# A retention kernel with two mixtures of experts: raw weights of expert 0 loaded one at a time and split row by row, mixed x kept one step later

## Chip, cores and metric

The kernel runs on one core of a Trainium2 chip. The metric is the time of one execution on the device in microseconds (us); lower is better. The engines are TensorE (PE, with its weight loads as PEld), VectorE (DVE), ScalarE (ACT), GpSimd (POOL) and SyncE (SP, which here only starts transfers).

## What is computed

Three stages on 2304 tokens of width 512: a retention layer (attention with a decay per head, without softmax), a dense mixture of 4 experts, and a mixture of 8 experts of which each token takes one.

```python
scores = scale * np.matmul(q, k.transpose(0, 1, 3, 2))
Dmat = np.where(rel >= 0, gamma[:, None, None] ** rel[None, :, :], 0.0)
x = np.matmul(scores * Dmat, v)                 # 4 x 8 heads x 576 x 64, then 2304 x 512
for e in range(4):                              # first mixture, dense
    out += p[:, e:e + 1] * (np.maximum(x @ w1[e], 0.0) @ w2[e])
for e in range(8):                              # second mixture, one expert a token
    out[mask] = gate_w[mask, None] * eom[mask, e, None] * (np.maximum(x[mask] @ w1[e], 0.0) @ w2[e])
```

All inputs and outputs are float32; the large matmuls run as sums of float16 products, each operand split into a high and a low part.

## The kernel before

**Retention.** 4 sequences of 9 chunks of 64 tokens make 36 steps s. A step (`at_step`, L394) has four groups of small matmuls on PE: the product with the state (L300), the scores of the next step (L277), the scores times v (L309) and what the next state gains (L324). DVE makes from them the masked scores `pf` (L282), the new state `sn` (four rows, L341, or one copy, L336) and x, as `xf` (L358). There is one PSUM buffer for scores (`sc`) and one for products (`uo`), so PE's next L277 waits for `pf`, and its next L300 for `xf`. `at_parts` splits `xf` into a high (ACT, L365) and a low part (POOL, L366) in `xo`. POOL also makes `ks`, the scaled keys (L256).

**Token blocks.** Four steps fill a block b of 256 tokens, of which there are 9. `x_mix` (L373, POOL, two calls of two rows) forms differences of x in place; `x_keep` splits them into `xm` (ACT L384, POOL L385; one buffer for each half, or straight into `xc` for blocks 0 and 1), and `x_store` writes parts to DRAM from POOL (L390, L392). `ago(s, b)` counts the steps since block b was filled; mixing falls on 1 and 2, keeping on 3 and 4, each with its store.

**Expert 0 in blocks 0 to 4.** A block has four units of the first layer (`l1_first`, L559, 24 matmuls into `ph`, then `ht` on ACT L545 and DVE L546) and four of the second (`l2`, L711, 12 matmuls into `po`). In blocks 1 to 3 the list has 8 units u = 0 to 7, l1 first; block 0 has only its four l2 units (its l1 is in the opening), block 4 only its four l1 units (its l2 goes with block 5). Behind each unit stands a call of `at_hook` (one retention step; in block 0 two behind every second unit), then `w_plan`. From block 5 on, and for experts 1 to 3, a scheme with 7 products of half size is used (`l1_mixed`, `l2_mixed`), for which the weights are mixed too.

**The weights.** Raw weights of an expert are eight loads of 128 x 1024 float32 (0.5 MB each, `w_load`, on SP) into four buffers `wr`: 0 to 3 of w1, 4 to 7 of w2. For the early blocks they are loaded and split once at the start (`w_split`; the form `split` uses ACT and DVE, `split_p` ACT, ACT and POOL). For the scheme of block 5 they are loaded again and go through a list of steps, `w_todo`, one taken by `w_do` behind each unit: `mix` writes a difference or sum back to `wr` (ACT L487 to a PSUM tile `pz`, DVE L488), `put` splits a quarter (ACT L219 to `pz`, ACT L220, DVE L221). The two k in the lists are two rows of blocks of a weight: k = 0 of w1 needs loads 0 and 2, k = 1 loads 1 and 3; of w2 4 and 6, then 5 and 7. Before, the list starts behind (0, 2) with the loads of w1 as two steps, 12 steps of w1 with k alternating, an empty step, two steps of loads of w2 and 10 steps of w2.

**What sets the order.** Up to L1208 the program's order holds on each engine. From L1209 on a scheduler orders each engine's instructions by what they depend on; `tc.issue_after` holds an instruction behind a named one of its engine. Each engine runs its own list in order and waits where an operand isn't there.

## Time and profile before

| | before |
|---|---|
| median of 3 runs | 1001.67 us (999.87 to 1007.35) |
| the profiled execution | 1003.75 us, of which 1001.9 are the span from first to last instruction |
| PE busy | 963.7 us (96%) |
| DVE, ACT, POOL busy | 574.1, 535.7, 421.2 us |
| mean granted TensorE clock | 0.992 |
| DMA | 209.49 MB, 209 GB/s in the mean |

The page cuts the span into 40 slices and gives each engine's busy share in tenths:

```profile
PE   6988999999999999999999999999999999999994
PEld 5565667899999999999999999999987677777773
DVE  5664572466667777766777675888888111211210
ACT  3354463667758777766777686676642122221211
POOL 4677674555556234455342454342322221112111
PEclk9999999999999999999999999999999999999997
DMA  9687884336556777457668726888834616654690
```

A slice is 25 us. A 9 is 90% or more. In the first six slices all engines and the DMA engines are in use; later PE alone is full. A wait is shown in brackets behind an instruction, with what released it; "issue" means that nothing in the profile accounts for it.

### The profile page before, as it was taken

To read this page: it belongs to the slowest core of one execution; us is meant where nothing else is said; L and a number is where in the kernel's file an instruction comes from. 1 tells how busy PE (TensorE), PEld (TensorE's weight loads), DVE (VectorE), ACT (ScalarE), POOL (GpSimd) and SP (SyncE) were. 2 spreads that over 40 slices of the span, in tenths; PEclk is the share of its full clock that TensorE was granted. 3 is DMA by queue.
4 is the path that set the end of the run, shared out by engine and by line. 5 is a ranking of instruction groups with operands and counts; after the bars stand their busy time and mean duration, and the time that the engine had idled before them with its cause. 6 is when DMAs were issued, how large, how long until landed. Compare 5 with 4: busy or idle time off the path is not lost. (4 is left out here: it accounts for less than half of the span.)

```text
span 1001.9 us, 31931 instructions
## 1 busy us (share of the span) xinstructions
PE 963.7 (96%) x13507; PEld 827.1 (83%) x13507; DVE 574.1 (57%) x1290; ACT 535.7 (53%) x1019; POOL 421.2 (42%) x446
## 2 busy tenths in 40 slices
PE   6988999999999999999999999999999999999994
PEld 5565667899999999999999999999987677777773
DVE  5664572466667777766777675888888111211210
ACT  3354463667758777766777686676642122221211
POOL 4677674555556234455342454342322221112111
PEclk9999999999999999999999999999999999999997
DMA  9687884336556777457668726888834616654690
GB/s 353 232 307 248 280 283 170 112 103 199 165 185 193 246 258 252 155 191 215 205 198 306 258 77 169 255 211 235 228 122 189 232 43 229 216 206 162 256 387 34
DMA packets 96052, 209.49 MB, mean 209 GB/s; under 512 B 21598, under 2 KB 42334, under 8 KB 93600
## 3 DMA queue, kind: packets, MB, share of 16 engines
q1 hardware_dynamic: 82784, 159.20, 47.7%
q0 software_dynamic: 13120, 48.20, 15.1%
q8 instruction: 108, 1.77, 0.7%
q14 instruction: 40, 0.33, 0.1%
HBM read 197.88 MB, written 52.99 MB: 250 GB/s over the span
## 5 line engine op out<-in xcount | busy, mean ns | idle before, releaser
L672 PEld LDWEIGHTS <-op 128*128 128x128 f16 x2604 | 245.7, 98 | 26.0 <-POOL s L211 0.7
L606 POOL TENSOR_TENSOR op<-sm,op 128x512 f16<-128x512 f32 x124 | 142.3, 1159 | 225.8 <-ACT op L605 225.7
L587 PEld LDWEIGHTS <-wm_a 128*128 128x128 f16 x3264 | 192.8, 98 | 3.9
L587 PE MATMUL ph<-xc,wm_a 128*128 128x128 f16 x2112 | 132.2, 219 | 0.0
L605 ACT ACTIVATE op<-sm 128x512 f16<-128x512 f32 x124 | 77.5, 634 | 86.6 <-DVE sm L610 85.1
L1094 DVE SCALAR_TENSOR_TENSOR h_s<-p_h,h_s 128x512 f16<-128x512 f32 x40 | 27.7, 691 | 159.5 <-ACT h_s L1093 159.5
L1101 PE MATMUL p_y<-wm_a,h_s 128*128 128x512 f16 x480 | 107.2, 379 | 0.5 <-DVE h_s L1094 0.5
L672 PE MATMUL pv<-wm_a,op 128*128 128x256 f16 x792 | 97.4, 273 | 0.0
L672 PE MATMUL px<-wm_a,op 128*128 128x256 f16 x744 | 91.3, 272 | 0.7 <-DVE acc L680 0.7
L1101 PEld LDWEIGHTS <-h_s 128*128 128x128 f16 x480 | 46.7, 98 | 52.3 <-DVE h_s L1094 0.7
L221 DVE TENSOR_TENSOR s<-pz,s 128x512 f16<-128x512 f32 x111 | 73.9, 682 | 15.6 <-ACT s L220 15.6
L1104 POOL DMA_INDIRECT out_dram<-y_s,sidxm x17 | 17.3, 1019 | 146.3 <-ACT y_s L1103 129.2
L587 PEld LDWEIGHTS <-wm_b 128*128 128x128 f16 x1296 | 76.9, 98 | 1.4
L219 ACT ACTIVATE pz<-sr 128x512 f32<-128x512 f32 x111 | 65.6, 605 | 15.0 <-DVE rk L830 7.9
L490 POOL TENSOR_TENSOR wr<-wr 128x512 f32<-128x512 f32 x48 | 60.5, 1271 | 29.8 <-ACT pz L219 29.1
L1093 ACT ACTIVATE h_s<-p_h 128x512 f16<-128x512 f32 x40 | 23.9, 597 | 79.6 <-PE p_h L1084 75.4
L220 ACT ACTIVATE s<-pz 128x512 f16<-128x512 f32 x111 | 64.0, 599 | 0.6
L1103 ACT ACTIVATE y_s<-p_y,x_g 128x512 f32<-128x512 f32 x20 | 13.7, 687 | 92.5 <-PE p_y L1101 78.9
L680 DVE SCALAR_TENSOR_TENSOR acc<-px,p_sb,acc 128x256 f32<-128x256 f32 x124 | 59.1, 476 | 6.8 <-PE px L672 6.5
L1084 PEld LDWEIGHTS <-wm_b 128*128 128x128 f16 x1056 | 59.9, 98 | 3.3 <-issue 1.1
L1084 PE MATMUL p_h<-x_s,wm_b 128*128 128x128 f16 x1056 | 61.6, 219 | 0.7 <-issue 0.7
L221 DVE TENSOR_TENSOR wm_a<-pz,wm_a 128x512 f16<-128x512 f32 x62 | 42.0, 688 | 34.7 <-ACT wm_a L220 34.3
(231 smaller groups left out, 1814.7 us busy)
## 6 DMA issues: line engine op xcount, KB each, us to landing
wm_a<-w2d SPq DMA_DIRECT2D x20, 2048.0 KB
wr<-in_w_dram SPq DMA_DIRECT2D x40, 512.0 KB
wm_b<-w1d SPq DMA_DIRECT2D x10, 2048.0 KB
wm_a<-w1d SPq DMA_DIRECT2D x10, 2048.0 KB
sr<-in_w1s_dram SPq DMA_DIRECT2D x64, 256.0 KB
w1d<-s SPq DMA_DIRECT2D x64, 256.0 KB
sr<-in_w2s_dram SPq DMA_DIRECT2D x64, 256.0 KB
w2d<-s SPq DMA_DIRECT2D x64, 256.0 KB
```

The source lines that it names most:

```text
L219: act.activation(out=z, in_=raw, func=ACTF.Copy, scale=scale)
L220: act.activation(out=hi, in_=z, func=ACTF.Copy)
L221: dve.tensor_tensor(out=lo, in0=z, in1=hi, op=ALU.subtract)
L490: pace["pool"] = pool.tensor_tensor(out=quarter(e, n, k, to), in0=quarter(e, n, k, x), in1=quarter(e, n, k, y), op=op)
L587: pe.matmul(bank[:, i], lhsT=w[:, k, u, 128 * i:128 * i + 128], rhs=x[:, v, d, k], start=(first and i == 0 and n == 0), stop=(n == 5), ski ...
L605: act.activation(out=hi, in_=s, func=ACTF.Copy)
L606: pool.tensor_tensor(out=lo, in0=s, in1=hi, op=ALU.subtract)
L672: pe.matmul(out, lhsT=o[a][:, v, k], rhs=w[c][:, k, u], start=(first and n == 0), stop=(n == 11), skip_group_check=True,)
L680: step = dve.scalar_tensor_tensor(out=a, in0=src, scalar=p_sb[:, b * TB + i, e:e + 1], in1=a, op0=ALU.mult, op1=ALU.add)
L1084: pe.matmul(ph[:, j], lhsT=w[k][:, x, f * 128:(f + 1) * 128], rhs=xs[:, y, k], start=(n == 0), stop=(n == 3 * KD - 1),)
L1094: dve.scalar_tensor_tensor(out=lo, in0=ph, scalar=0.0, in1=hi, op0=ALU.max, op1=ALU.subtract)
L1101: pe.matmul(po, lhsT=h[:, a, k], rhs=w[k][:, b], start=(n == 0), stop=(n == 3 * KF - 1))
```

## The change

Four things are changed. Expert 0's steps of w1 and w2 run all of k = 0 and then all of k = 1. Its eight raw loads are no longer steps of the list: `RAW_AT` names for each the unit behind which it is asked for, and the list of 22 steps starts behind (1, 4). `x_keep` and the stores behind it move from 3 and 4 steps after a block's last to 4 and 5 (the hook runs to one step more, with two calls behind (4, 3)). And in the opening, the split of the second row of w2 moves ahead of two retention steps.

```diff
--- before.py
+++ after.py
@@ -511,14 +511,16 @@
                 lambda q=q: q(0, 4),
                 lambda q=q: q(2, 6),
             ]
-        return [f for pair in zip(*rows) for f in pair]
+        return rows[0] + rows[1] if e == 0 else [f for pair in zip(*rows) for f in pair]
 
     def w2_steps(e):
         steps = []
 
+        late = []
+
         def both(*what):
             for k in range(2):
-                steps.append(lambda k=k: [w(k) for w in what])
+                (late if k and e == 0 else steps).append(lambda k=k: [w(k) for w in what])
 
         q = lambda i, c: lambda k: put(e, 1, k, i, c)
         m = lambda to, x, y: lambda k: mix(e, 1, k, to, x, y, ALU.subtract)
@@ -533,7 +535,7 @@
         both(q(3, 2), m(2, 2, 3))
         both(q(1, 4))
         both(q(2, 6))
-        return steps
+        return steps + late
 
 
     hts = {}
@@ -1195,11 +1197,11 @@
     w_split(0, KD)
     at_split(NS + 1)
     l1_first(0, 1, 1, 2)
+    w_split(0, KD + 1, split_p)
     later_step(NS)
     at_scores(NS + 1)
     l1_first(0, 2, 1, 2)
     later_step(NS + 1)
-    w_split(0, KD + 1, split_p)
     at_split(NS + 2)
     l1_first(0, 3, 1, 2)
     w_split(0, KD + 2)
@@ -1232,7 +1234,7 @@
 
     def at_hook():
         s = nxt[0]
-        if s >= NSTEP + 4:
+        if s >= NSTEP + 5:
             return
         nxt[0] += 1
         if s + 4 < NSTEP:
@@ -1265,13 +1267,13 @@
             if n == 2:
                 x_store(b, 0)
                 x_mix(b, 1)
-            if 2 < n < 5:
-                x_keep(b, n - 3)
+            if 3 < n < 6:
+                x_keep(b, n - 4)
                 if b > 1:
-                    x_store(b, n - 1)
-            if b < 2 and n == 5:
+                    x_store(b, n - 2)
+            if b < 2 and n == 6:
                 x_store(b, 1)
-        if s == NSTEP + 3:
+        if s == NSTEP + 4:
             at_ctx.close()
             wm["b"] = ctx.enter_context(tc.tile_pool(name="w_b", bufs=1)).tile([128, 6, 2048], F16, name="wm_b")
             later["raw"] = ctx.enter_context(tc.tile_pool(name="raw_s", bufs=3))
@@ -1308,13 +1310,19 @@
                 pend_store.append(s_split(i - 2, f))
         s_at[0] = i + 1
 
+    RAW_AT = {(0, 3): 0, (1, 1): 2, (1, 3): 1, (1, 5): 3, (2, 3): 4, (2, 5): 6, (3, 0): 5, (3, 2): 7}
+
     def w_plan(e, b, u):
 
         if e == 0 and b < BM:
-            if (b, u) == (0, 2):
-                w_todo.extend([w_loads(0, 0, 2), w_loads(0, 1, 3)] + w1_steps(0) + [lambda: None])
-                w_todo.extend([w_loads(0, 4, 6), w_loads(0, 5, 7)] + w2_steps(0))
-            w_do()
+            if (b, u) == (0, 3):
+                w_todo.extend(w1_steps(0) + w2_steps(0))
+            i = RAW_AT.get((b, u))
+            if i is not None:
+                with tc.issue_after(pace["sp"].ins):
+                    w_load(0, i)
+            if (b, u) >= (1, 4):
+                w_do()
         elif e < 3 and b >= (2 if e else BM):
             if (b, u) == (2 if e else BM, 0):
                 w_tiles(e + 1)
@@ -1417,7 +1425,7 @@
                     with tc.issue_after(pace["pool"].ins):
                         x_load((b + 1) % NB, pool)
                 if e == 0:
-                    for _ in range(1 + (b == 0 and u % 2)):
+                    for _ in range(1 + (b == 0 and u % 2 or (b, u) == (BM - 1, 3))):
                         at_hook()
                 if not last:
                     w_plan(e, b, u)
```

In SP's list, the start of the second raw loading (`wr<-in_w_dram`; `qkr` and `vkr` are the inputs of a retention step) before:

```order
L450 DMA wr<-in_w_dram 128x1024 x2
L248 DMA vkr<-in_vk_dram 128x640
L242 DMA qkr<-in_qk_dram 128x640 x2
L450 DMA wr<-in_w_dram 128x1024
L248 DMA vkr<-in_vk_dram 128x640
L450 DMA wr<-in_w_dram 128x1024
L248 DMA vkr<-in_vk_dram 128x640
L242 DMA qkr<-in_qk_dram 128x640 x2
L248 DMA vkr<-in_vk_dram 128x256
```

and after:

```order
L450 DMA wr<-in_w_dram 128x1024
L248 DMA vkr<-in_vk_dram 128x640
L242 DMA qkr<-in_qk_dram 128x640
L248 DMA vkr<-in_vk_dram 128x640
L242 DMA qkr<-in_qk_dram 128x640
L450 DMA wr<-in_w_dram 128x1024
L248 DMA vkr<-in_vk_dram 128x256
L242 DMA qkr<-in_qk_dram 128x640
L248 DMA vkr<-in_vk_dram 128x640
L242 DMA qkr<-in_qk_dram 128x512
L450 DMA wr<-in_w_dram 128x1024
```

The four loads that stood among two steps' inputs now stand one by one among the inputs of several; the first of them is where the third was.

In ACT's list, around the end of block 1's units (`xm_` with a number is one half of one block's mixed x: 1617 and 1616 are block 3's before, 1663 the first half of block 3 after), before:

```order
L219 ACTIVATE pz<-wr 128x512
L384 ACTIVATE xm_1617<-xf 128x512
L365 ACTIVATE xo<-xf 128x4x64
L384 ACTIVATE xm_1616<-xf 128x512
L220 ACTIVATE wm_a<-pz 128x512
L219 ACTIVATE pz<-wr 128x512
L220 ACTIVATE wm_a<-pz 128x512
```

and after:

```order
L384 ACTIVATE xm_1396<-xf 128x512
L487 ACTIVATE pz<-wr 128x512 x3
L365 ACTIVATE xo<-xf 128x4x64
L219 ACTIVATE pz<-wr 128x512
L220 ACTIVATE wm_a<-pz 128x512
L487 ACTIVATE pz<-wr 128x512
L219 ACTIVATE pz<-wr 128x512
L365 ACTIVATE xo<-xf 128x4x64
L384 ACTIVATE xm_1663<-xf 128x512
L220 ACTIVATE wm_a<-pz 128x512
```

The first half of block 3 stands one retention step later, behind an `xo` and with one L220 behind it instead of four rows of x and weights; block 2's second half (1396) and the first steps of the weight list have come into the rows ahead of it.

In DVE's list, from the unit (2, 3) on (the `ht` row is its first), before:

```order
L546 SCALAR_TENSOR_TENSOR ht<-ph,ht 128x512
L282 TENSOR_TENSOR pf<-sc,ka 128x256
L206 SCALAR_TENSOR_TENSOR wg_sb<-wgr,wg_sb 128x64
L341 SCALAR_TENSOR_TENSOR sn<-sn,ka,uo 128x64 x4
L358 TENSOR_TENSOR xf<-uo,ka 128x4x64
L221 TENSOR_TENSOR wm_a<-pz,wm_a 128x512
L282 TENSOR_TENSOR pf<-sc,ka 128x256
L341 SCALAR_TENSOR_TENSOR sn<-sn,ka,uo 128x64 x4
L358 TENSOR_TENSOR xf<-uo,ka 128x4x64
```

and after, from the second row behind that unit's `xf`:

```order
L221 TENSOR_TENSOR wm_a<-pz,wm_a 128x512
L488 TENSOR_TENSOR wr<-pz,wr 128x512
L221 TENSOR_TENSOR wm_a<-pz,wm_a 128x512
L282 TENSOR_TENSOR pf<-sc,ka 128x256
L221 TENSOR_TENSOR wm_a<-pz,wm_a 128x512
L341 SCALAR_TENSOR_TENSOR sn<-sn,ka,uo 128x64 x4
L358 TENSOR_TENSOR xf<-uo,ka 128x4x64
L221 TENSOR_TENSOR wm_a<-pz,wm_a 128x512
```

Between the `xf` of one step and that of the next stood one L221; now four rows of the weight steps stand there (and the gate weights' L206 ahead of them), and one more behind.

## Rows read from the trace of the kernel before

**Rows 1.** Stretches: busy us of each engine, granted clock, DMA share, GB/s.

```profile
50.00:75.00 25.00, 21.63 (x467) 16.77 (x458) 15.19 (x46) 12.91 (x26) 19.08 (x28) 0.93 0.86 307
...
400.00:450.00 50.00, 50.00 (x683) 47.46 (x682) 35.35 (x60) 35.36 (x68) 26.23 (x25) 1.00 0.53 176
```

**Rows 2.** PE's timeline, 30 to 68 us: start, us, operation, [wait <-releaser].

```profile
34.69 0.59 PE L711 MATMUL po<-wm_c,ht 128*128 128x512 f16 x2 [0.83 <-POOL wm_c L139]
...
37.19 0.46 PE L277 MATMUL sc<-qkr 64*64 64x64 f32 x16 [0.48 <-DVE pf L282]
...
54.14 0.33 PE L309 MATMUL uo<-pf,vkr 64*64 64x64 f32 x5 [1.35 <-issue]
...
62.48 0.40 PE L300 MATMUL uo<-qkr,sn 64*64 64x64 f32 x11 [1.94 <-issue]
...
63.69 1.46 PE L559 MATMUL ph<-xc,wm_c 128*128 128x256 f16 x6
...
67.16 0.82 PE L559 MATMUL ph<-xc,wm_a 128*128 128x256 f16 x6
```

**Rows 3.** Instruction queue's packets in 51.75:52, 60:60.25, 63.5:63.75: count, MB, share.

```profile
q8 instruction: 1, 0.02, 24.2%
...
q8 instruction: 1, 0.02, 25.1%
...
q8 instruction: 1, 0.02, 38.5%
```

**Rows 4.** A stretch behind the second "issue" wait, columns as rows 1.

```profile
64.00:66.00 2.00, 2.00 (x11) 1.35 (x10) 1.96 (x7) 0.42 (x1) 1.66 (x4) 0.50 0.96 257
```

**Rows 5.** PE's timeline, 85 to 154 us.

```profile
85.60 0.46 PE L277 MATMUL sc<-qkr 64*64 64x64 f32 x16 [2.67 <-DVE pf L282]
...
86.35 0.46 PE L309 MATMUL uo<-pf,vkr 64*64 64x64 f32 x16 [0.29 <-DVE xf L358]
...
86.98 4.45 PE L711 MATMUL po<-wm_a,ht 128*128 128x512 f16 x12
...
119.80 0.46 PE L300 MATMUL uo<-qkr,sn 64*64 64x64 f32 x16 [1.08 <-DVE xf L358]
...
139.26 0.46 PE L300 MATMUL uo<-qkr,sn 64*64 64x64 f32 x16 [0.57 <-DVE xf L358]
...
141.16 0.46 PE L277 MATMUL sc<-qkr 64*64 64x64 f32 x16 [0.74 <-DVE pf L282]
142.36 2.75 PE L711 MATMUL po<-wm_c,ht 128*128 128x512 f16 x12 [0.73 <-DVE wr L488]
...
153.16 0.46 PE L300 MATMUL uo<-qkr,sn 64*64 64x64 f32 x16 [0.71 <-DVE xf L358]
```

**Rows 6.** Timelines of ACT (two rows), POOL and SP (two rows).

```profile
28.80 0.42 ACT L139 ACTIVATE xc<-xf 128x256 f16<-128x256 f32 x1 [2.53 <-DVE xf L139]
...
81.43 0.63 ACT L384 ACTIVATE xm<-xf 128x512 f16<-128x512 f32 x1 [2.94 <-DMA xcd<-xm]
...
74.97 0.68 POOL L392 DMA_DIRECT2D xcd<-xm  x1 [0.30 <-POOL xm L385]
...
43.81 1.64 SPq L450 DMA_DIRECT2D wr<-in_w_dram  x2
...
51.44 0.45 SPq L450 DMA_DIRECT2D wr<-in_w_dram  x1
```

**Rows 7.** Groups by line, 40 to 168 us: count, busy us, mean ns, idle before.

```profile
L373 POOL TENSOR_TENSOR xf<-xf 128x256 f32<-128x256 f32 x35 | 26.6, 760 | 4.2 <-DVE xf L358 3.1
...
L341 DVE SCALAR_TENSOR_TENSOR sn<-sn,ka,uo 128x64 f32<-128x64 f32 x84 | 17.8, 273 | 3.4 <-PE uo L324 3.2
...
L385 POOL TENSOR_TENSOR xm<-xf,xm 128x512 f16<-128x512 f32 x13 | 15.2, 1177 | 6.7 <-ACT xm L384 6.6
...
L221 DVE TENSOR_TENSOR wm_a<-pz,wm_a 128x512 f16<-128x512 f32 x14 | 9.6, 686 | 8.0 <-ACT wm_a L220 7.8
```

**Rows 8.** Transfers that write or read x's parts in DRAM, 40 to 170 us.

```profile
DMA to landing us min/median/max: 2.5/5.3/8.6
```

## Prediction

> **What bounds the kernel now.** I read the stretches first. From 200 us on TensorE (PE) is busy without a gap (400 to 450: 50.00 of 50); only the opening and the first five token blocks leave it idle, 3.4 us in 50 to 75 [rows 1]. The change moves work in those blocks alone, so its gain is at most the idle time there. The program's order on PE differs in three places by one group of rows; what changes is when the others serve it. I then listed, in PE's timeline, every wait between 30 and 157 us with its releaser [rows 2, 5], and asked of each whether the change moves what it waits for. A unit is one step of block b's l1 or l2 list, written (b, u), followed by one retention step; a pair takes about 3.85 us.
>
> The waits: 0.83 and 0.48 at 34 to 37 us; 1.35 and 1.94 "issue" at 54 and 62; 2.67 and 0.29 at 85.6; 1.08 at 119.8; 0.57, 0.74, 0.73 and 0.71 at 139 to 153 [rows 2, 5]. Two of them cost more: behind the 1.94 the granted clock is 0.50 (1.2 of 2.4 GHz) [rows 4], and behind the 2.67 the matmuls are as slow. Four groups of six lasted from 63.69 to 67.98, 4.3 us, where a group at full clock takes 0.7 from start to start (1.5 lost); the 12 of 86.98 took 4.45, those of 142.36 2.75 (1.7 lost) [rows 2, 5]. After 1.35 and 1.08 the clock stayed. All of it together is 11.4 + 3.2 = 14.6 us: no version of this change can give more.
>
> **The change part by part.**
>
> *Second row of w2 split earlier.* PE waits 0.83 for POOL's low half of wm_c, then 0.48 for DVE's mask product, which stands behind the late splits [rows 2]. ScalarE (ACT) now makes it ahead of two retention parts, in a hole of 2.53 us before 28.80 [rows 6]. Both waits go: **-1.3**.
>
> *Raw weights one by one.* Before, four raw loads of 0.5 MB stand on SP between 43.81 and 51.44 us [rows 6]; now, by the rows that they stand beside, one is asked for near 50, one near 57, the others near 69 and 77. So about 1 MB less is under way when PE waits on "issue". What those waits are: 125 matmuls and as many weight loads lie between the two, and each was preceded by one packet of the instruction queue, at 51.75 and 60.00; PE went on 2.4 and 2.5 us after it [rows 2, 3]. The second packet came 5.9 us after PE had gone on from the first; the next one, with the load ebbing, 1.0 us after 62.48. A block lasts PE 6.4 us here, so a packet that starts within 4.0 us is in time. At the 307 GB/s of that stretch [rows 1] 1 MB is 3.3 us: 5.9 becomes 2.6, or 4.3 if only half of it lay ahead of the packet. I take the first wait as gone (**-1.35**), 0.4 left of the second and the clock kept (1.94 - 0.4 + 1.5 = **-3.0**). From below: nothing, if the delay doesn't hang on the bytes.
>
> The Trainium skill ("Runtime: NRT & Kernel Launch", Instruction fetch mechanics) says that the sequencer refills in blocks of 256 instructions and that a crossing is mostly hidden; the spacing agrees with the trace, the hiding doesn't. It also says ("DMA: Bandwidth & Descriptors", Queues, rings and completion order) that an engine takes turns between its queues packet by packet, so a fetch would not stand behind another queue's backlog; the 5.9 us speak against it. By that rule 4.35 us of my sum would fall away.
>
> *Weight steps from (1, 4), first row of blocks first, and mixed x one step later.* These decide the rest, since ACT, DVE and POOL run their queues in order.
>
> End of block 1. Before, ACT's activate of xm stood 2.94 us, until 81.43, for a store of the block before that POOL issued at 74.97 [rows 6]; three weight rows behind it delayed DVE's pf, and PE stood 2.67, then ran slow. Now the heavy steps start here: the three L488 delay one xf by 0.5, and PE waits 0.45. The xm row still waits, with fewer rows behind it. POOL makes both xm of block 2 in a row (2 x 1.16), then issues both stores (from 76.1 on before's clock); the mixing of x stands behind them and ends at 82.3; the store lands 5.3 after its issue, at 81.4 [rows 7, 8]. So xm starts near 82.4, and with L220, L221 and pf PE goes on 2.25 later, at 84.65, having wanted to at 83.35: 1.3, then 0.29 as before. Waits of 1.35 kept the clock. Before 2.67 + 0.29 + 1.7 = 4.65, now 0.45 + 1.3 + 0.3 = 2.05: **-2.6**.
>
> End of block 2. In (2, 0) an xm row stands ahead of the weight step: 0.6 later, less a slack of 0.2, makes 0.45. Behind (2, 3) DVE has, between two xf that PE needs, L206, three L221, one L488, pf, four sn and xf: start to start 0.6 each for the large ones (0.69 with the end), 0.35, 0.8, 0.4, in sum 4.5 [rows 7], plus 0.7 of waiting for ACT, which serves four steps in a row, against PE's 3.85: PE waits 1.2. The next xf is behind the L221 that follows xm of block 5, and that xm waits for POOL: xm, store, xm, store (two times 1.16 + 0.3 + 0.68), four mixing rows of 0.76 and three others of about 0.65 [rows 6, 7]. It ends 10.5 after (2, 3), xf follows at 13.1, and PE, which would start at 12.6, waits 0.65. New 2.3, old 1.08 (a raw weight asked for late, now five units early): **+1.2**.
>
> End of block 3. The four old waits, 2.75, came from (3, 2) and (3, 3), each with xm and a mixing step; in the new order xm of (3, 2) is in (3, 3), whose step has no mixing, and these waits go. But the second row's mixing steps now stand in (3, 5) to (3, 7). Behind (3, 3) DVE has three L221, two L488, pf, sn and xf, with ACT late by 0.8: xf 8.8 after (3, 3), PE wants it at 7.75: 1.2. Then two L488, of which the second reads ACT's row behind xm, which POOL's chain frees at 9.95; ACT's four rows and DVE's L488, pf, L221, sn, xf bring xf to 14.85 against 12.8: 2.15. That is between the 1.94 and the 2.67 after which the clock fell, so I add 1.6. New 4.95, old 2.75: **+2.2**. If those xf come in time, it is -2.75 instead.
>
> *At no cost.* The weight steps are 22 as before, done by (4, 1); block 4's l1 units have no retention step, and two DVE rows more lie beside 2.6 us of matmuls each. The one step more at the end is a second call in (4, 3). The last stores come about 1 us later; SP's loads of the next stage wait for them, but PE has no wait there; without that cover 1 us. The raw loads 4 to 7 find their buffers read, so SP isn't held.
>
> **Sum.** -1.3 - 1.35 - 3.0 - 2.6 + 1.2 + 2.2 = -4.85 us. Against the profiled execution (1003.75, a span of 1001.9) that is 998.9; the median of the runs shown is 1001.67, 2.1 lower, and the same gain on it gives **996.8**.
>
> **The rivals.**
> 1. *The new queues hold.* The waits behind (2, 3) and (3, 3) are sums of many starts on three queues; if each queue is some 0.1 us a row faster than I count, they vanish. Then 1.3 + 1.35 + 3.4 + 2.6 + 1.1 + 2.75 = 12.5: **989.2**. For: rows lie closer than their busy times add up to, and three of the four waits are below 1.3. Against: DVE's rows alone, 4.5, are above PE's 3.85.
> 2. *The fetch delay does not hang on the raw loads.* Both "issue" waits stay with the slow clock: 0.5 gained, **1001.2**. For: qkr, vkr and the stores of x still load the engines. Against: the 1.0 us when they ebbed.
> 3. *Slower: xm stores land late.* Two stores are issued together, a raw load beside them; at the longest landing, 8.6 instead of 5.3 [rows 8], xm starts 2.3 later at the end of block 1, 0.9 at block 2's, 1.5 at block 3's, 4.7 in all, and the clock falls at the first two as well (1.7 + 1.6): -4.85 + 8.0 = +3.1, **1004.8**. It decides from a landing of 6.2 us on, where the store and no longer POOL's mixing frees xm. For: the old 2.94 was such a wait, 6.5 after its issue. Against: the median.
>
> **How the numbers follow.** My forecast has 0.46, rival 1 0.17, rival 2 0.20, rival 3 0.13, anything else 0.04. A measurement of this kernel tells about 1% from no change, here 991.7 and 1011.7. Faster by over 1% needs over 10 us, which only rival 1 reaches: 0.17. Slower by over 1% needs rival 3 and a lost fetch and more: 0.02. Within 1%: 0.81. The range reaches down to 988, where most of rival 1 is in, and up to 1004: rival 2 and the milder half of rival 3.
>
> **What would show it.** No wait of PE at 34 to 37 us; "issue" waits of PE before 70 us under 0.7 in sum; no granted clock of 0.50 in the slices of 50 to 100 us; at the end of block 1 one wait for pf of about 1.3 behind ACT's xm; two waits for xf behind (2, 3) and two behind (3, 3), the last the longest. I am wrong if the "issue" waits stay, if the raw load shows up as the releaser of L487, or if PE waits after 175 us, where nothing should change.

## The result and the profile after

The changed kernel takes 1012.81 us in the median (four runs, 1009.38 to 1014.80) against 1003.56 for the kernel before (also four runs, 999.87 to 1007.35). The ratio of the means is 1.0088, with a 95% interval from 1.0062 to 1.0114. It is slower by a little under 1%. Forecast were 996.8 us and a range up to 1004.0; the time lies outside it, on the other side. The profiled execution of the changed kernel is the fastest of its four, 1009.38 us with a span of 1007.6, 5.6 us above the profiled execution before.

The change added two lines ahead of L545, so what was L559 and L711 is L561 and L713 here. Stretches of the changed kernel, columns as in [rows 1]:

```profile
50.00:75.00 25.00, 21.04 (x473) 16.96 (x463) 11.55 (x38) 9.02 (x19) 16.45 (x25) 0.93 0.81 269
...
400.00:450.00 50.00, 50.00 (x682) 47.44 (x680) 34.86 (x60) 37.88 (x73) 27.56 (x27) 1.00 0.57 183
```

Late in the kernel nothing has changed: PE is full, as in [rows 1]. In 50 to 75 us it is idle for 4.0 us, where it was idle for 3.4, with fewer rows of DVE and ACT beside it. PE's timeline of the changed kernel behind 31 us, the rows with a wait of over 0.5 us (and the one behind the last of them):

```profile
62.59 0.72 PE L300 MATMUL uo<-qkr,sn 64*64 64x64 f32 x13 [3.87 <-DVE xf L358]
...
86.30 0.48 PE L277 MATMUL sc<-qkr 64*64 64x64 f32 x16 [2.80 <-DVE pf L282]
...
106.03 0.46 PE L324 MATMUL uo<-vkr,ks 64*64 64x64 f32 x15 [1.26 <-issue]
...
119.09 0.46 PE L300 MATMUL uo<-qkr,sn 64*64 64x64 f32 x16 [2.30 <-DVE xf L358]
...
151.27 0.46 PE L300 MATMUL uo<-qkr,sn 64*64 64x64 f32 x16 [1.18 <-DVE xf L358]
...
158.56 0.71 PE L300 MATMUL uo<-qkr,sn 64*64 64x64 f32 x16 [3.43 <-DVE xf L358]
...
160.05 3.56 PE L713 MATMUL po<-wm_a,ht 128*128 128x512 f16 x12
```

The waits of [rows 2] at 34 and 37 us are gone, and so are both "issue" waits at 54 and 62. At the instruction of the second stands the longest wait of all, 3.87 us behind (1, 1), of which the prediction has no word; it doesn't hide a late fetch, since the packet of the instruction queue came at 55.75 (60.00 before) and PE was idle only from 58.72, 3.0 us later (in the kernel before PE went on 2.5 us after its packet). The wait at the end of block 1 is as long as in [rows 5], 2.80 against 2.67. That behind (2, 5) is 2.30 where there was 1.08, and behind (3, 6) there are 3.43 and a row of 3.56 us where such a row takes 2.76. The clock behind three of these waits:

```profile
62.60:64.60 2.00, 2.00 (x64) 1.91 (x64) 1.02 (x2) 0.78 (x2) 2.00 (x5) 0.53 0.48 172
...
119.00:121.00 2.00, 1.91 (x53) 1.33 (x54) 0.00 (x0) 1.12 (x3) 1.18 (x3) 1.00 0.95 350
...
158.50:161.00 2.50, 2.44 (x51) 1.81 (x52) 0.84 (x2) 1.30 (x3) 0.67 (x1) 0.50 0.02 7
```

It is at its lower level (1.2 GHz) behind the 3.87, for nearly all of the 2 us shown, and behind the 3.43, and at 2.4 GHz behind the 2.30.

Where the time went is read from the starts of the units in both timelines of PE. "Step" is what the difference grows by from one place to the next, and beside it stands what the prediction had there:

| from, to | before starts at | after starts at | difference | step | forecast |
|---|---|---|---|---|---|
| start, first l1 row of the opening's second half | 21.82 | 23.33 | +1.51 | +1.51 | 0 |
| to (1, 0) | 51.03 | 51.14 | +0.11 | -1.40 | -1.3 |
| to (1, 1) | 57.50 | 55.92 | -1.58 | -1.69 | -1.35 |
| to (1, 4) | 72.82 | 72.98 | +0.16 | +1.74 | -3.0 |
| to (2, 0) | 92.45 | 92.83 | +0.38 | +0.22 | -2.6 |
| to (3, 0) | 124.45 | 127.29 | +2.84 | +2.46 | +1.2 |
| to (4, 0) | 157.34 | 164.17 | +6.83 | +3.99 | +2.2 |
| to the end of the span | 1001.9 | 1007.6 | +5.7 | -1.1 | 0 |

The first step lies ahead of every instruction that the change touches, in a stretch in which the DMA engines are full. In this profile of the changed kernel the opening's l1 starts 0.7 us later (14.50 against 13.77), and the granted clock in 15 to 20 us is 0.67 where it was 1.00. In the profiles of this study that row starts between 21.08 and 23.73 us, whatever the kernel. The next two steps came near the forecast. The miss is in the four below them, and the experiments take them in turn. The table explains these two executions, which lie 5.6 us apart; the medians lie 9.25 us apart, and no trace shows where the rest stands.

### The profile page after: what moved, and what is told of

Its sections match the earlier page's. It is cut to its first block, busy times and chain, and to the rows that moved or that the text cites. A ratio compares the mean times of both kernels' runs of the same rounds, so it can differ in the third digit from the quotient of the medians.

```text
span 1007.6 us, 31932 instructions
## 1 busy us (share of the span) xinstructions
PE 963.5 (96%) x13507; PEld 828.5 (82%) x13507; DVE 575.0 (57%) x1290; ACT 535.2 (53%) x1019; POOL 420.7 (42%) x446
## 5 line engine op out<-in xcount | busy, mean ns | idle before, releaser
L221 DVE TENSOR_TENSOR s<-pz,s 128x512 f16<-128x512 f32 x111 | 74.0, 683 | 16.2 <-ACT s L220 16.2
L219 ACT ACTIVATE pz<-sr 128x512 f32<-128x512 f32 x111 | 65.7, 605 | 14.9 <-DVE rk L832 8.8
L220 ACT ACTIVATE s<-pz 128x512 f16<-128x512 f32 x111 | 63.9, 598 | 0.6
L221 DVE TENSOR_TENSOR wm_a<-pz,wm_a 128x512 f16<-128x512 f32 x62 | 42.0, 688 | 37.5 <-ACT wm_a L220 37.1
```

The lines of the kernel that those rows point to most:

```text
L219: act.activation(out=z, in_=raw, func=ACTF.Copy, scale=scale)
L220: act.activation(out=hi, in_=z, func=ACTF.Copy)
L221: dve.tensor_tensor(out=lo, in0=z, in1=hi, op=ALU.subtract)
```

## The experiments

Ratios are to the kernel before, timed on the same chip between the runs.

| run | kernel | ratio | 95% interval |
|---|---|---|---|
| the change | | 1.0088 | 1.0062 to 1.0114 |
| e1 | changed, x_keep not late | 1.0027 | 1.0007 to 1.0047 |
| e2 | before, x_keep late | 1.0084 | 1.0055 to 1.0112 |
| e3 | changed, x_keep not late in blocks 0 and 1 | 1.0056 | 1.0036 to 1.0076 |
| e4 | before, early split | 0.9981 | 0.9958 to 1.0004 |
| e5 | changed, xm in more buffers | 1.0031 | 1.0014 to 1.0048 |
| e6 | e5, xf in three buffers | 0.9990 | 0.9974 to 1.0007 |
| e7 | e1, xm in more buffers | 0.9891 | 0.9865 to 0.9917 |
| e8 | e4, xm in more buffers | 0.9952 | 0.9929 to 0.9974 |
| e9 | e7, w1's raw loads in pairs | 0.9926 | 0.9903 to 0.9950 |
| e10 | e1, raw load 3 later | 1.0024 | 1.0001 to 1.0046 |
| e11 | e7, raw load 3 later | 0.9912 | 0.9889 to 0.9934 |
| e12 | e7, two POOL rows more | 0.9950 | 0.9932 to 0.9968 |
| e13 | e7, four transfers more | 0.9954 | 0.9936 to 0.9971 |
| e14 | changed, xm behind L220 | 1.0009 | 0.9992 to 1.0027 |
| e15 | e6, xm behind L220 | 0.9895 | 0.9860 to 0.9929 |
| e16 | e7, xm behind L220 | 0.9921 | 0.9894 to 0.9947 |
| e17 | e1, xm behind L220 | 0.9908 | 0.9874 to 0.9941 |
| e18 | e4, xm behind L220 | 0.9911 | 0.9876 to 0.9946 |

### The parts alone: e1 to e4

My theory after reading the trace was that the late x_keep makes the loss through the two buffers of xf: the first xf of block 3 goes into the buffer of block 1, and the second x_keep of block 1, which reads that buffer, now falls into the same step. DVE, ACT and POOL of the changed kernel, ahead of the wait of 3.87:

```profile
62.02 0.42 DVE L358 TENSOR_TENSOR xf<-uo,ka 128x256 f32<-128x256 f32 x1 [4.67 <-POOL xc L385]
...
55.43 0.62 ACT L384 ACTIVATE xc<-xf 128x512 f16<-128x512 f32 x1
...
57.46 0.61 POOL L256 TENSOR_TENSOR ks<-vkr,ka 128x256 f32<-128x256 f32 x1 [1.47 <-DMA vkr<-in_vk_dram]
58.03 0.73 POOL L373 TENSOR_TENSOR xf<-xf 128x256 f32<-128x256 f32 x1
...
60.12 0.67 POOL L390 DMA_DIRECT2D xcd<-xo  x1
60.76 1.22 POOL L385 TENSOR_TENSOR xc<-xf,xc 128x512 f16<-128x512 f32 x1
```

DVE stands 4.67 us for POOL's half of x_keep. ACT had made its half at 55.43, but on POOL a late vkr, the mixing of block 2 and a store stand ahead. e1 undoes the late x_keep in the changed kernel:

```diff
-            if 3 < n < 6:
-                x_keep(b, n - 4)
+            if 2 < n < 5:
+                x_keep(b, n - 3)
                 if b > 1:
-                    x_store(b, n - 2)
-            if b < 2 and n == 6:
+                    x_store(b, n - 1)
+            if b < 2 and n == 5:
                 x_store(b, 1)
```

(and the hook ends one step earlier, without the second call behind (4, 3)).

> The changed kernel with one part undone: x_keep and its stores fall on 3 and 4 steps after a block's last again; the single raw loads, the order of the weight steps, their start behind (1, 4) and the opening stay changed. Theory A (late keep): there are two xf buffers, and the first xf of block b+2 goes into that of block b. One step later, the second x_keep of block b falls in the very step that writes that xf, so DVE's L358, and with it PE, waits for POOL's L385. It expects no wait of PE for xf behind (1, 1), no 0.50 clock there, a time 5 to 8 us under the changed kernel's: ratio to before 0.996 to 1.002. Theory B (weight steps): the loss comes from the steps packed behind (1, 4) and the order of rows, whatever x_keep does: ratio 1.006 to 1.010, the waits at the ends of blocks 1 to 3 unchanged.

e2 is the reverse, the kernel before with these lines as after.

> The kernel before with one part of the change alone: x_keep and its stores on 4 and 5 steps after a block's last. Theory A (late keep holds the xf buffer): a new wait of PE for xf behind (1, 1) of 2 to 4 us whose releaser on DVE is POOL's L385, then a stretch at half clock; ratio to before 1.004 to 1.009. Theory B (weight steps): no such wait, ratio 0.998 to 1.002.

e3 takes the late step from blocks 0 and 1 alone (`late = b > 1`, and `2 + late < n < 5 + late`).

> The changed kernel with x_keep back on 3 and 4 steps for blocks 0 and 1 alone (they keep into xc); blocks 2 and later stay one step later. Theory A: the wait of 3.87 us at 62.59 us and the slow clock behind it go, those at 86, 119 and 158 us stay: 4 to 6 us under the changed kernel, ratio to before 1.002 to 1.005. Theory B: at most 1 us gained, ratio 1.007 to 1.010.

e4 moves the one line of the opening:

```diff
     l1_first(0, 1, 1, 2)
+    w_split(0, KD + 1, split_p)
     later_step(NS)
...
     later_step(NS + 1)
-    w_split(0, KD + 1, split_p)
```

> The kernel before with one part of the change alone: the second row of w2 split ahead of two retention steps in the opening. My prediction's term: PE's two waits of 0.83 and 0.48 at 34 to 37 us go and nothing takes their place: -1.3 us, ratio 0.9987. Rival: the gain is taken back by the next wait (the issue wait at 54 us, set by a fetch that starts by the queue's own time): ratio 1.000.

The late x_keep alone (e2) costs 0.84%, as much as the whole change, and the rows are those of theory A: DVE's xf waits 5.41 us for POOL's L385 and PE 4.83 behind (1, 1).

```profile
64.34 0.42 DVE L358 TENSOR_TENSOR xf<-uo,ka 128x256 f32<-128x256 f32 x1 [5.41 <-POOL xc L385]
```

In e3 PE has no wait there, and the time falls by 0.32%, somewhat less than I expected; in e1 by 0.6%. So the buffer of xf is a cause. It is not the only one: e1, without the late step, is still 0.27% above the kernel before. These shares don't add up to the whole, since one wait can stand behind several causes. The early split measured -0.19%, 1.9 us, with an interval that reaches no change; its two waits are gone in the trace. Each trace is one execution: in e4, which differs from the kernel before in the opening alone, the wait behind (2, 5) is 3.24 where 1.08 was, so a single wait is not yet the price of an edit.

### More buffers: e5 to e8

At the ends of the blocks another wait comes first. ACT, DVE and POOL of the changed kernel before PE's 2.80:

```profile
78.56 0.60 ACT L219 ACTIVATE pz<-wr 128x512 f32<-128x512 f32 x1 [0.27 <-DVE wm_a L221]
...
84.08 0.63 ACT L384 ACTIVATE xm<-xf 128x512 f16<-128x512 f32 x1 [4.58 <-DMA xcd<-xm]
84.61 0.58 ACT L220 ACTIVATE wm_a<-pz 128x512 f16<-128x512 f32 x1
...
85.22 0.69 DVE L221 TENSOR_TENSOR wm_a<-pz,wm_a 128x512 f16<-128x512 f32 x1 [5.77 <-ACT wm_a L220]
85.83 0.41 DVE L282 TENSOR_TENSOR pf<-sc,ka 128x256 f32<-128x256 f32 x1
...
74.64 2.27 POOL L385 TENSOR_TENSOR xm<-xf,xm 128x512 f16<-128x512 f32 x2
76.86 1.38 POOL L392 DMA_DIRECT2D xcd<-xm  x2
...
81.26 1.81 POOL L373 TENSOR_TENSOR xf<-xf 128x256 f32<-128x256 f32 x2
```

The first store was issued at 76.86 and landed by 84.08, 7.2 us later, where I had reckoned with 5.3; POOL's mixing ends at 83.07, 1.0 earlier. To take the store's part away, e5 gives xm other buffers; a tile of the pool of `ht` has the same size, and there are ten in rotation:

```diff
-            xos[b][1] = [at_1.tile([128, 2, 2, 2, HB], F16, name="xm" + str(h), bufs=1) for h in range(2)]
+            xos[b][1] = [ht_p.tile([128, 2, 2, 2, HB], F16, tag="ht", name="xm") for h in range(2)]
```

> The changed kernel with one line more: the two halves of xm are taken from the pool of ht (ten buffers of the same size in rotation) instead of one buffer each, so no ACT L384 has to wait for a store to land. Theory A1 (stores landing late make the ends of blocks 1 and 3 long): ACT's waits of 4.58 and 3.92 us for the store of xm go; POOL's mixing, which ends 1.0 and 1.3 us before those stores land, releases L384 instead, so PE's 2.80 at the end of block 1 becomes about 1.8 and the 3.43 behind (3, 6) about 2.1; the 3.87 behind (1, 1) stays. 2 to 4 us under the changed kernel, ratio to before 1.004 to 1.007. Rival A2 (the rows of weight steps on ACT and DVE make these waits, whatever the stores do): ratio 1.008 to 1.010.

e6 uses the room for a third xf (`name="xf", bufs=3`).

> The kernel of e5 with a third buffer for xf (in the room that xm left). Theory A: the only reason for the 3.87 us behind (1, 1) is that the first xf of block 3 goes into the buffer of block 1; with three it goes elsewhere, the wait and the slow clock behind it go: another 4 to 6 us, ratio to before 0.999 to 1.003. Rival: POOL's queue of mixing, stores and ks is late there anyway and ks or xo become the releaser: under 2 us more than e5, ratio over 1.003.

> The kernel of e1 (the changed one without the late x_keep) with xm from the pool of ht. In e1 ACT's L384 waits 6.34 us for a store of xm at the end of block 1 and 4.56 at the end of block 3, where POOL's mixing ends 2.5 and over 4 us earlier. Theory A1: those waits shrink to under 3 us each, and PE's 4.49 and 3.44 to under 2.2 each: 4 to 8 us under e1, ratio to before 0.995 to 0.999. Rival A2 (rows of weight steps): within 2 us of e1, ratio 1.001 to 1.004.

> The kernel of e4 (before with the early split alone) with xm from the pool of ht: what the single buffer of xm costs in the kernel before. ACT's wait of 2.94 us for the store at 81 us goes, POOL's mixing ends about 1 us earlier there: theory A1 expects 1 to 3 us under e4, ratio to before 0.995 to 0.998; rival A2 none, 0.998.

e5 gains 0.57% on the change, 5.7 us where 2 to 4 were expected. ACT and PE of e5 at the end of block 1:

```profile
83.00 0.63 ACT L384 ACTIVATE xm<-xf 128x512 f16<-128x512 f32 x1 [3.92 <-POOL xf L373]
...
85.23 0.46 PE L277 MATMUL sc<-qkr 64*64 64x64 f32 x16 [1.78 <-DVE pf L282]
```

As theory A1 said, the mixing takes the store's place as releaser, and PE's 2.80 becomes 1.78. In e6 there is no wait behind (1, 1), and it gains another 0.41%: the buffer of xf a second time, in another way than e3. e8 came as expected, 2.9 us under e4. But e7 came out far below its expectation, 0.9891, though it differs from e6 only by the step of x_keep and the third xf. ACT and PE of e6 show what is left:

```profile
78.84 0.63 ACT L384 ACTIVATE xm<-xf 128x512 f16<-128x512 f32 x1 [5.71 <-POOL xf L373]
79.38 0.58 ACT L220 ACTIVATE wm_a<-pz 128x512 f16<-128x512 f32 x1
...
81.06 0.71 PE L277 MATMUL sc<-qkr 64*64 64x64 f32 x16 [3.78 <-DVE pf L282]
```

No buffer holds anything here, and PE waits 3.78. Two things differ from e7: POOL makes both xm of block 2 directly ahead of the mixing of block 3, and on ACT xm stands between L219 and L220. In e7 the scheduler has put it behind that L220, and in e8 too:

```profile
76.66 0.60 ACT L220 ACTIVATE wm_a<-pz 128x512 f16<-128x512 f32 x1
...
80.32 1.15 ACT L384 ACTIVATE xm<-xf 128x512 f16<-128x512 f32 x2 [2.76 <-POOL xf L373]
```

These are rows of e7. So the gains of e7 and e8 are those of buffer and place together, and e5 to e8 don't tell the causes apart.

### POOL's work ahead of the mixing: e12

e12 puts that POOL work back into e7 without moving x_keep:

```diff
         m = xfs[b]
+        if i == 0 and b > 1:
+            for _ in range(2):
+                more = at_1.tile([128, 2, 2, HB], F32, name="more", bufs=1)
+                pool.tensor_tensor(out=more, in0=m[:, 0], in1=m[:, 1], op=ALU.subtract)
```

> The kernel of e7 (no late x_keep, xm in more buffers) with two POOL rows of 128x512 more directly ahead of each block's mixing from block 2 on (their results are used by nothing): the work that the late x_keep brings to that place, 2 x 1.16 us, without moving x_keep and without any buffer held longer. Theory P (POOL's chain: what stands ahead of the mixing makes xm late on ACT, and with it the weight rows behind it, DVE's pf and xf, and PE): PE's waits at the ends of blocks 1, 2 and 3, 0.28, 1.38 and 1.21 us in e7, grow by 1.5 to 2.3 us each, with a slow clock behind one or two of them: 4 to 9 us over e7, ratio to before 0.993 to 0.998. Rival P2 (the late x_keep costs by its held buffers and its later stores alone, POOL has room): within 2 us of e7, ratio under 0.992.

ACT and PE of e12 at the ends of blocks 1 and 3 (its L388 and L377 are L384 and L373 elsewhere):

```profile
75.48 0.60 ACT L220 ACTIVATE wm_a<-pz 128x512 f16<-128x512 f32 x1
81.41 1.15 ACT L388 ACTIVATE xm<-xf 128x512 f16<-128x512 f32 x2 [5.03 <-POOL xf L377]
...
142.16 1.15 ACT L388 ACTIVATE xm<-xf 128x512 f16<-128x512 f32 x2 [4.39 <-POOL xf L377]
...
147.51 0.46 PE L300 MATMUL uo<-qkr,sn 64*64 64x64 f32 x16 [2.80 <-DVE xf L358]
```

The time lies where theory P put it, and yet the rows contradict it at two of three places. xm waits 5.03 us at the end of block 1, nearly as in e6, and PE doesn't wait there at all; at the end of block 2 it waits 1.15 once, where e7 has 0.98 and 1.38. Only at the end of block 3 does it wait longer, 1.45 and 2.80; and a part of the time is in the "issue" waits from 45 to 70 us, 1.86 where e7 has 0.60. A late mixing is not enough, then. What is different at the end of block 1 is that L220 stands ahead of xm.

### The place of xm on ACT: e14 to e18

e14 is the changed kernel with its own buffers. The calls of x_keep, with their stores, are put off until the unit's weight step has been issued, and L384 is held behind that step's L220:

```diff
-        act.activation(out=hi, in_=z, func=ACTF.Copy)
+        pace["z"] = act.activation(out=hi, in_=z, func=ACTF.Copy)
...
-        with tc.issue_after(pace["act"].ins):
+        with tc.issue_after(pace.get("z", pace["act"]).ins), tc.issue_after(pace["act"].ins):
...
-                x_keep(b, n - 4)
+                kept.append(lambda b=b, n=n: x_keep(b, n - 4))
...
                     w_plan(e, b, u)
+                    while kept:
+                        kept.pop(0)()
```

> The changed kernel with the same buffers, but the rows of x_keep (and its stores) are put behind the unit's weight step, and ACT's L384 behind that step's last L220. In the changed kernel ACT has L219, xm, L220 at the end of block 1, and xm waits 4.58 us for a store, with L220, DVE's L221, pf and PE behind it. Theory Q (it is this place on ACT that hands xm's wait to PE): PE's 2.80 at 86 us falls under 0.8 with no slow clock behind it, the 2.30 and the 3.43 behind (2, 5) and (3, 6) fall by 1 us or more each; the 3.87 behind (1, 1), another cause, stays. 4 to 8 us under the changed kernel, ratio to before 1.001 to 1.005. Rival Q2 (DVE's and ACT's rows of weight steps make the waits, wherever xm stands): ratio 1.007 to 1.010.

> The same edit on the kernel of e6 (the changed one with xm and xf in more buffers), where ACT's xm waits 5.71, 5.54 and 3.48 us for POOL's mixing and PE 3.78, 3.00 and 2.99 behind it. Theory Q: these three waits of PE fall by 2 us or more each, the time to 0.991 to 0.995 of before, 4 to 8 us under e6. Rival Q2: within 2 us of e6, 0.997 to 1.001.

> The same edit on the kernel of e7 (no late x_keep, xm in more buffers), where the scheduler has put xm behind L220 at the end of block 1 already. Theory Q: only the ends of blocks 2 and 3 can gain, 1.38 and 1.21 us at the most: ratio 0.987 to 0.990. Rival Q2: 0.989 to 0.992, since xm and its stores come later.

> The kernel of e1 (the changed one without the late x_keep, the buffers of before) with xm's rows behind the unit's weight step, as in e14. In e1 ACT's xm waits 6.34 and 4.56 us for stores of xm and PE 4.49 and 3.44 behind it. Theory Q: those two waits of PE fall under 1.5 us each, and there is no wait for xf behind (1, 1), which the late x_keep of e14 leaves: 3 to 8 us under e14 and 4 to 10 under e1, ratio to before 0.992 to 0.998. Rival (without more buffers the stores hold xm so long that the next rows are late wherever it stands): over 1.000.

> The kernel of e4 (before with the early split alone) with xm's rows behind the unit's weight step. Theory Q: the kernel before had the same place on ACT, and its 2.67 us with the slow clock behind it at the end of block 1 (3.36 in e4) and the wait behind (2, 5) come from it in part: 2 to 6 us under e4, ratio to before 0.992 to 0.996, and the single raw loads are worth the rest of what e17 has. Rival: nothing gained, 0.998, since there the L220 are fewer behind xm.

ACT, DVE and PE of e14 at the end of block 1:

```profile
77.65 0.60 ACT L220 ACTIVATE wm_a<-pz 128x512 f16<-128x512 f32 x1
...
83.05 0.63 ACT L384 ACTIVATE xm<-xf 128x512 f16<-128x512 f32 x1 [4.50 <-POOL xf L373]
...
78.28 0.69 DVE L221 TENSOR_TENSOR wm_a<-pz,wm_a 128x512 f16<-128x512 f32 x1
78.97 0.42 DVE L282 TENSOR_TENSOR pf<-sc,ka 128x256 f32<-128x256 f32 x1
...
81.99 0.46 PE L277 MATMUL sc<-qkr 64*64 64x64 f32 x16
```

For the end of block 1 this settles it. xm waits 4.50 us (now for the mixing), as long as in the changed kernel (4.58, for the store), but pf is made at 78.97 and PE goes on at 81.99 with no wait. At the end of block 2 xm waits 5.02, longer than the 2.27 of the changed kernel, and PE 0.98 where it had 2.30. At the end of block 3 the wait for the store is itself shorter (1.97 for 3.92), so there the place is not shown to be all of it. The edit brings 0.8% of the 0.88% back, with every load, buffer and weight step of the change in place. It moves more than ACT's row: POOL's half of x_keep and its stores go behind the weight step too. Two waits of PE for xf remain, 3.28 us behind (1, 1) and 2.64 behind (3, 1). At both DVE's xf waits for POOL's L385, first for xc and then for xm of block 3, whose buffer the first xf of block 5 needs. In e15, where that buffer is free too, both are gone and PE has few waits left, although ACT's xm waits 6.9 us at the end of block 1. ACT's waits for xm in the stretch from 60 to 160 us of the changed kernel, grouped (sum, times, longest):

```profile
ACT xm L384 <- DMA xcd<-xm: 8.5, 2, 4.6
...
ACT xm L384 <- POOL xf L373: 2.3, 1, 2.3
```

and of e15 in 60 to 150 us, with PE's waits from 40 to 170 us below:

```profile
ACT xm L384 <- POOL xf L373: 12.5, 3, 6.9
```

```profile
PE uo L324 <- issue: 2.0, 2, 1.8
PE uo L300 <- DVE xf L358: 1.6, 3, 0.9
PE po L713 <- ACT xm L384: 1.2, 1, 1.2
```

10.8 us of xm's waiting went with a ratio of 1.0088, 12.5 us with 0.9895. The nearest comparison is e6, which differs from e15 by this edit alone: three waits of xm of 14.7 us in sum, and 0.9990. That ACT, DVE and POOL take their rows strictly in order is what the Trainium skill says too ("PSUM — Partial Sum Buffer", Engine vs sequencer instructions); e14 agrees, since the wait stayed and only what stood behind it changed.

e17, the change without the late x_keep and with xm behind L220, has 0.9908 with the buffers of before; e18, the kernel before with the early split and the same place of xm, has 0.9911. Both beat both kernels by about 0.9% or more. e14, e15, e17 and e18 came out a little faster than the ranges expected. e17 differs from e1 by this edit alone and takes 1.2% less; of the two waits that were to fall under 1.5 us, that at the end of block 1 is gone and that at the end of block 3 is 1.75. All that tells e17 from e18 are the single raw loads, the order of rows and the later start, and between these two they are worth nothing that can be measured. Between e7 and e8 they are worth 0.6%. So their gain is between nothing and 6 us, and what it depends on stays open. e16 missed theory Q's range and gained nothing over e7 (0.9921 and 0.9891, intervals that overlap): there the place was right at the end of block 1 already, and PE's waits at the ends of blocks 2 and 3 (1.16, 0.87 and 1.61 where e7 has 0.98, 1.38 and 1.21) didn't shrink in sum.

### What the raw loads do to the fetch: e9, e10, e11, e13

e9 asks for w1's four raw loads as before the change, two behind (0, 2) and two behind (0, 3), in e7.

> The kernel of e7 with one edit undone: the four raw loads of w1 are asked for as before the change, two behind (0, 2) and two behind (0, 3); the order of weight steps, their start and w2's loads stay as changed. Theory F (the instruction fetch of PE is late when raw loads fill the DMA queues): the two issue waits of PE near 54 and 62 us come back, 1.5 to 3.5 us in sum where e7 has 0.6, and the time rises by as much: 1.5 to 5 us over e7, ratio to before 0.991 to 0.994. Rival F2 (the fetch delay does not hang on the raw loads, the second rival of the prediction): the issue waits before 70 us stay under 0.8 in sum, ratio within 0.001 of e7's 0.989.

e13 leaves the single loads and adds other transfers where the four stood:

```diff
+            if (b, u) in ((0, 2), (0, 3)):
+                with tc.issue_after(pace["sp"].ins):
+                    for i in range(2):
+                        sp.dma_start(out=dram.tile([128, 1024], F32, name=f"more{u}{i}"), in_=w1[0, :, i])
```

> The kernel of e7 with four more transfers of 0.5 MB on SP's queue (w1 to a scratch in DRAM that nothing reads), two behind (0, 2) and two behind (0, 3), where the raw loads stood before the change; the raw loads themselves stay single. Theory F (what stands in the DMA queues makes PE's instruction fetch and the retention step's loads late): PE's waits for issue, qkr and ks between 45 and 70 us, 0.60 us in e7, grow to 2.5 us or more: 2 to 6 us over e7, ratio 0.991 to 0.995. Rival F2: under 1.0 us of such waits, ratio within 0.0015 of e7's 0.989.

PE's timeline of e13:

```profile
54.77 0.33 PE L309 MATMUL uo<-pf,vkr 64*64 64x64 f32 x5 [1.57 <-issue]
...
64.37 0.40 PE L300 MATMUL uo<-qkr,sn 64*64 64x64 f32 x11 [3.07 <-issue]
```

They are the two rows of [rows 2], at the same two instructions, 4.64 us in sum where e7 has 0.60: what stands in the DMA queues does delay the fetch. e9 alone didn't show it. Its issue waits are 0.54 us, under the 0.8 of rival F2; a wait of 1.31 for qkr stands beside them, and its time is 0.35% above e7, in theory F's range, with intervals that overlap. Over all profiles the issue waits between 45 and 70 us sum to 3.29, 1.35, 2.87, 1.86, 0.54 and 0.7 where the loads come in pairs (before, e2, e4, e8, e9, e18; 1.8 in the mean; in e2 the wait of 4.83 for xf stands where the second would), and to 0.3 in the mean of the 13 where they come singly (0 in eight, 1.86 at the most, in e12). So the effect is real, and the profiled execution of before shows it at its largest.

The last two ask whether raw load 3, which is issued beside a store of xm, makes that store late (e10, in e1) or makes the fetch late at 87 us (e11, in e7). Both only move it in `RAW_AT` from (1, 5) to (2, 0).

> The kernel of e1 with the raw load 3 asked for behind (2, 0) instead of (1, 5). In e1 it is issued at 71.80 us, 0.16 us behind the start of the store of xm (71.64) that lands only at 79.64 and holds ACT for 6.34 us. Theory G (the raw load beside the store makes it late): the store lands by 78.5 or earlier, ACT's wait falls to 5.2 or less, PE's 4.49 to 3.4 or less: 1 to 3 us under e1, ratio 0.9995 to 1.002. Rival G2 (other transfers, the loads of wgr, kb, k16 and xc just ahead, make it late): the wait stays over 5.8, ratio 1.002 to 1.0035.

> The kernel of e7 with the raw load 3 asked for behind (2, 0) instead of (1, 5), a try at a still faster version: e7 has an issue wait of 0.98 us at 87 us and one of 0.28 at 80 us, behind that load. If the load is their cause (theory F) they go, ratio 0.988 and below; if not, 0.989.

In e10 the store landed 7.1 us after its issue instead of 8.0, ACT's wait fell from 6.34 to 5.62 and PE's from 4.49 to 3.62; the time is e1's. The load is a part of it at the most; the other transfers of that stretch were not taken away. In e11 the wait of 0.98 is gone and another of 0.85 stands at 64 us, and 2.58 at 146; nothing is gained.

## Why the prediction was wrong

Two steps failed. "Mixed x one step later" was put at nothing behind (1, 1): the sum had no wait for a buffer of xf, and 3.87 us of PE with the slow clock stand there, so that the stretch to (1, 4), put at -3.0, became +1.74. The end of block 1, put at -2.6, became +0.22: the sum took "fewer rows behind" xm for a short wait of PE, and 2.80 us came instead of 1.3, since the one row behind it was L220, on which L221 and with it pf wait. The ends of blocks 2 and 3 had the right sign and were too small by about 3 us together.

**Second row of w2 split earlier: right.** -1.3 was forecast and the step to (1, 0) is -1.40; e4 measured 1.9 us, with an interval from 4.2 us gained to 0.4 lost.

**Raw weights one by one: the mechanism right, the size too large.** Both issue waits went, and e13 brings them back with nothing but bytes in the queue. But the 4.35 us were read from one execution. 1.8 us of issue waits is the mean of six profiles with pairs, another fetch, at 106 us, now waits 1.26 instead of 0.25, and the kernels with and without this part differ by nothing (e17, e18) to 0.6% (e7, e8). What delays the fetch at 106 us is open: no raw load is asked for there between 78 and 104.7 us, and e18, with none near either, waits 1.21 at the same instruction. Rival 2 fell for the two waits it spoke of: they do hang on the transfers.

**Behind (1, 1): a wait that the prediction has not.** The steps "weight steps and mixed x one step later" were costed at the ends of blocks 1 to 3 alone, by the order of rows on three engines. What an operand's buffer is waiting for was looked at for xm and not for xf. The part on x_keep would have had to ask who needs the buffer that x_keep reads; with two xf the answer is the first step of block b+2, and the late x_keep lies exactly there. Its price is the 3.87 with the slow clock behind it, where 1.94 with the slow clock went: +1.74 in place of -3.0. e3 and e6 measure it as 0.32% and 0.41%, and e2 shows the same wait without the rest of the change.

**End of block 1: +0.22 instead of -2.6.** The sum had every piece: xm waits for the later of store and mixing, then L220, L221 and pf. It took 5.3 us for the store, the median of [rows 8]; it was 7.2, beyond the 6.2 that rival 3 named as its point of decision, and the mixing was 0.8 late too (vkr came late for POOL's ks, 1.95 us). 1.3 became 2.80, and a wait of that length had the slow clock behind it again. The sentence that misled is "with fewer rows behind it": one row behind xm is enough if it is L220, and e14 shows that with that row ahead of xm the landing would not have mattered.

**End of block 2: near.** One wait of 2.30, behind (2, 5), and one of 0.42 stand where I had 2.3 in three; none came behind (2, 4). The rest of the step is the fetch of 1.26, which the sum didn't have.

**End of block 3: right in kind, too small.** I had 1.2 and 2.15 with a slow clock; 1.18 and 3.43 with a slow clock came, the second behind an xm that waited 3.92 us for its store, where I had POOL's chain as what frees it.

**Small slips of the sum.** Two waits at the end of block 3 and one of block 2 are written 0.1 to 0.15 larger than the two times beside them give (8.8 against 7.75 is 1.05, not 1.2): 0.4 us in all, which changes nothing above.

**The rivals and the chances.** Rival 3, slower through late stores, had the right sign and 0.13; by its own terms it ended at 1004.8, since it lacked xf. Within 1%, to which 0.81 was given, is what the interval says nearly throughout. The range was too narrow above: it had no room for a wait of a kind that the sum did not contain, though a reordering on five queues makes such waits likely.

## What to carry to other kernels

Where an engine runs its rows in order, ask of a row that may wait not how long it waits but what stands behind it on that engine and who needs that: here a wait of 4.5 us on ACT cost PE 2.80 us and the slow clock or nothing, depending on whether the second half of a weight step stood behind or ahead of it, and the edit that puts it ahead at every block's end brought 0.8%. When a reader of a buffer is moved later, find the next writer of that buffer and the step in which it writes; a free slot in the order is not a free buffer. And a wait that hangs on the load of the DMA queues should be read from several executions before its whole length is booked as a gain.

## What I had not expected of the hardware

The length of PE's wait does not tell by itself whether the clock falls: it was 0.50 behind 1.94 us in the kernel before [rows 4] and 0.60 behind 2.64 us in e14, but 1.00 behind 2.30 us in the changed kernel and behind 2.99 us in e6. The stretches behind the waits in e14 and in e6:

```profile
129.80:132.00 2.20, 2.20 (x67) 1.93 (x68) 1.83 (x4) 2.20 (x5) 1.68 (x3) 0.60 0.52 123
...
153.90:156.00 2.10, 2.01 (x54) 1.38 (x55) 0.76 (x2) 1.39 (x3) 0.68 (x1) 1.00 0.04 8
```

Booking the slow clock by the wait's length, as the prediction did for each term, is off by up to 1.7 us a place.

What the DMA queues hold can make a fetch of PE's instructions late: four transfers of 0.5 MB turned 0.60 us of such waits into 4.64. The Trainium skill ("Runtime: NRT & Kernel Launch", Instruction fetch mechanics) calls the crossing from one block of instructions to the next mostly hidden. In the stretch from 45 to 70 us the profiles with single loads agree, with 0.3 us in the mean, and e13 doesn't. Later stretches of the same profiles have single "issue" waits up to 2.58 us (e11 at 146 us), whose cause no run here shows.
